# One token list instead of two in an attention, MLP and mixture-of-experts kernel, and three steps put elsewhere in its written order

## Chip, cores and metric

The kernel runs on one core of a Trainium2 chip, as one launch. The metric is the device time of one execution in microseconds (us); a lower time is better.

## Reference

Three layers follow one another on 4608 tokens of 512 numbers (8 sequences of 576 tokens, 8 heads of 64). The attention looks only inside chunks of 64 tokens.

```
scores = scale * q_c @ k_c^T;  attn = softmax(scores);  x = attn @ v_c      # chunks of 64
h = x @ w_in;  x = (s * relu(h)**2 + b) @ w_out                              # 512 -> 2048 -> 512
logits = x @ w_gate + modality_bias[modality_id];  e_idx = argmax(logits)
gate_w = softmax(logits)[e_idx]
for e in range(8):                                                           # 512 -> 1024 -> 512
    out[mask] = gate_w[mask] * (relu(x[mask] @ w1[e]) @ w2[e])
```

Everything is float32. The kernel reaches that precision by splitting numbers into a high and a low part and multiplying three times (high by high, high by low, low by high).

## The kernel before

**Tokens** go through attention and the first MLP in 18 blocks of 256 (`NB`), each two tiles of 128 (`NTB`). Blocks 0 and 1 run together in an opening stretch (functions `p_*`), in which the weights `w_in` and `w_out` also arrive and are split; blocks 2 to 17 run through `m_l1` (first matrix product) and `m_l2` (second), 16 column groups `f` each, the second two groups behind the first.

**The order is written by hand.** Inside `tc.manual_schedule` every engine executes its instructions in the order in which the Python code records them. An engine that waits for something therefore holds back all that was recorded behind it on that engine, ready or not. TensorE is PE in the profile, VectorE DVE, ScalarE ACT, GpSimd POOL; SyncE (SP) issues the ordinary DMAs.

**The opening.** Weight chunk `n` goes through `c_split` (ACT, two operations), `c_word` (DVE, three), `c_high` (ACT, writes the high part) and `c_low` (DVE, writes the low part). A token tile `i` goes through `a_transpose`, `a_scores`, `a_soft`, `a_norm`, `a_pt` and `a_pv`; `a_pv` multiplies by the values on PE (`pxt`), and ACT and DVE write the result's high and low part (`x`). After the hand-written opening a loop over steps `s` begins, whose step `s = 2` needs weight chunk 2 and, for its second half, tile 3's `x`.

**Choosing an expert.** For each block `j` `g_choose` (DVE, a dozen small operations ending in the one-hot `oh` and the running count `run`) takes the best of 8 logits. `g_rank` lets PE add up how many tokens chose each expert before (`prk`, five tiny products), `g_dest` (DVE) makes of it a row number, and `g_scatter` (POOL, two indirect DMAs, one for each token tile) writes each token's number into that row of a list in HBM. This is done one block behind, in group `f = 14` (`RANK`) and after it. For the last block the generator `routing()` does it, interleaved with the first expert units; its three steps are the logits' preparation, the choice, and then rank, scatter and the tables of units (`u_tables`, DVE).

**Two lists.** `ids` is a pair of lists, one for even and one for odd token tiles, with 8 x 4608 + 128 rows each. Both are filled with `HALF` = 2^19, and token t is written as t - 2^19; so the sum of the two entries of a row is the token's number, or 2^20 where no token is.

**Expert units.** A unit `u` is up to 128 tokens of one expert; units 0 to 3 are known early, and 41 units run here. `u_ids` (POOL) reads its 128 rows from both lists, `u_gather` (POOL) adds the two columns and gathers the tokens (`xg`), `u_x` transposes them on PE (`px`) and makes the scaled high and low parts on DVE (`scu`, `xf`, `xhl`), `u_l1(u, half)` is the first product (`pu`, with `hr` and `hh` behind it on DVE and ACT), `u_l2` the second (`po`), and an indirect DMA writes the rows (`out_dram`). `unit(u)` sets the order: `u_l1(u, 0)`, `u_x(u + 1)`, a step of `routing()`, `u_l1(u, 1)`, a step of `routing()`, gathers, `u_l2(u - 1)`. The scratch bank of PSUM that `px`, `plg` and `prk` use has two buffers.

The core of the order around the change:

```python
c_word(2); a_pv(3); c_high(2); c_split(3); p_relu(1); c_low(2)     # the opening
if f == RANK: g_rank(j - 1)                                        # blocks 2 to 16
l2_lag(j, f)
u_l1(u, 0); u_x(u + 1); next(route, None)                          # unit(u), u > 0
u_l1(u, 1); next(route, None)
```

Of the kernel before, what the change touches and what calls it, by code (L numbers as in the profile page):

```python
# [20 lines left out]


HALF = 1 << 19

# [6 lines left out]
def kernel(  # L31
# [58 lines left out]

    ids = [dram.tile([E * NT + P, 1], I32, name=f"ids{t}") for t in range(NTB)]
    wgt = dram.tile([E, DM], F32, name="wgt")
# [25 lines left out]
    tokid = const.tile([P, NTILE], I32, name="tokid")  # L118
    nc.gpsimd.iota(tokid, pattern=[[P, NTILE]], base=-HALF, channel_multiplier=1)
    eidx = iota("eidx", [P, E], [[1, E]])  # L120
# [37 lines left out]
    def small(n, shape, dt=F32, bufs=None):  # L158
        return sm.tile(shape, dt, tag=n, name=n, **({"bufs": bufs} if bufs else {}))
# [42 lines left out]
    def c_split(n):  # L202

        raw = craw[n]
        h, l = raw[:, :, 1], raw[:, :, 0]
        nc.scalar.activation(
            out=h.bitcast(F32), in_=h.bitcast(F32), func=AF.Copy, scale=2.0 ** -112
        )
        nc.scalar.activation(out=l, in_=l.bitcast(U32), func=AF.Copy, scale=2.0 ** -29)
# [24 lines left out]
    def c_low(n):  # L234
        hi, lo = c_dst(n)
        tt(lo, cwf.pop(n), hi.bitcast(F32), ALU.subtract)
# [421 lines left out]
    def g_scatter(j):  # L658
        di = rank.pop(j)
        for t in range(NTB):  # L660
            nc.gpsimd.indirect_dma_start(
                out=ids[t], out_offset=bass.IndirectOffsetOnAxis(ap=di[:, t, :], axis=0),
                in_=tokid[:, j * NTB + t:j * NTB + t + 1], in_offset=None,
            )
# [140 lines left out]
    def u_ids(u, idx):  # L805
        two = uid[u] = small("uid2", [P, NTB], I32, 6)
        for t in range(NTB):
            nc.gpsimd.indirect_dma_start(
                out=two[:, t:t + 1], out_offset=None, in_=ids[t],
                in_offset=bass.IndirectOffsetOnAxis(ap=idx, axis=0),  # L810
            )

    def u_gather(u):
        two = uid[u]
        uid[u] = small("uid", [P, 1], I32, 10)
        nc.gpsimd.tensor_tensor(out=uid[u], in0=two[:, 0:1], in1=two[:, 1:2], op=ALU.add)
        n = KNOWN_ROWS if u < NE else NT
        nc.gpsimd.indirect_dma_start(
            out=xg_t[u % 3], out_offset=None, in_=ys[:n],
            in_offset=bass.IndirectOffsetOnAxis(ap=uid[u], axis=0),  # L820
            bounds_check=n - 1, oob_is_err=False,
        )
# [284 lines left out]
    with tc.manual_schedule(engines=ENG):  # L1107
# [4 lines left out]
        none = su.tile([P, E * NTILE + 1], I32, tag="misc", name="none")  # L1112
        nc.vector.memset(none, HALF)
        a_load(0)
# [55 lines left out]
        c_word(2)  # L1170
        a_pv(3)
        c_high(2)
        c_split(3)
        p_relu(1)
        c_low(2)
        c_word(3)
# [6 lines left out]
        for s in range(2, NF + LEAD + LAG):  # L1183
# [44 lines left out]
            if s == 7:  # L1228
                nc.sync.dma_start(out=wg4, in_=w_gate.rearrange("(c p) e -> p c e", p=P))
                for t in range(NTB):  # L1230
                    nc.sync.dma_start(out=ids[t].rearrange("(p n) a -> p (n a)", p=P), in_=none)
            if s == 8:
# [38 lines left out]
    with tc.manual_schedule(engines=ENG):  # L1271
        for j in range(2, NB - 1):
            PREP, HIGH, STORE = PREP_2 if j == 2 else PREP5 if j < 8 else PREP4
            for f in range(NF):
                att_pe(j, f, 0)
                m_l1(j, f)
                att_pe(j, f, 1)
                if f == RANK:
                    g_rank(j - 1)
                l2_lag(j, f)  # L1280
                att_pe(j, f, 2)
                if f == (ROWS_2 if j == 2 else LAG - 1):
# [127 lines left out]
        def unit(u, lo, hi):  # L1410
            if u:
                u_l1(u, 0)
                if u + 1 < hi:
                    u_x(u + 1)
                next(route, None)
            u_l1(u, 1)
# [70 lines left out]
```

## Time and profile before

| | |
|---|---|
| Time, median of 3 runs | 1443.72 us (1437.5 to 1445.77) |
| Time of the profiled execution | 1438.02 us, span 1436.3 us |
| PE busy | 1394.2 us, 97% of the span |
| DVE busy | 1070.7 us, 75% |
| ACT busy | 724.1 us, 50% |
| POOL busy | 435.7 us, 30% |
| Granted PE clock, mean | 0.99 |

The span reaches from the first to the last instruction. An engine's row says how long it was executing; the rest it waited or had nothing to do. [...]

### The profile page before, as it was taken

The numbers are of one execution on the slowest core, as the hardware profiler recorded it, in microseconds if no ns is written. First come the engines' busy times: TensorE is split into PE (matmuls) and PEld (weight loads), VectorE is DVE, ScalarE is ACT, GpSimd is POOL, SyncE is SP. The second block draws the span as 40 slices with busy tenths as digits, with TensorE's granted clock in tenths as the row PEclk, the third lists the DMA queues.
The fourth block names the chain that finished last, engine by engine and source line by source line (L and its number), as shares of the span: only waits on it lengthen the run. The fifth ranks groups of instructions, "written<-read, shape, count | busy, mean of one in ns | idle before, by whom it ended". The sixth has DMA issues, their size and how long they took to land. (4 is left out here: it accounts for less than half of the span.)

```text
span 1436.3 us, 32039 instructions
## 1 busy us (share of the span) xinstructions
PE 1394.2 (97%) x11853; PEld 1151.0 (80%) x11853; DVE 1070.7 (75%) x2643; ACT 724.1 (50%) x1658; POOL 435.7 (30%) x515
## 2 busy tenths in 40 slices
PE   6899999999999999999999999998999999999995
PEld 5787888888888888888888888886767766776773
DVE  6987688877977977887697787767676676677662
ACT  4975555656565656655656565543233323333331
POOL 0000232332323333223323223463533433443320
PEclk9999999999999999999999999999999999999998
DMA  8673355555446443534534443461211231535340
GB/s 202 182 200 111 82 131 157 130 149 159 131 126 176 117 131 111 157 98 125 148 111 118 126 133 111 105 215 31 64 53 45 105 106 39 194 122 182 129 151 18
DMA packets 183886, 178.86 MB, mean 125 GB/s; under 512 B 131108, under 2 KB 139556, under 8 KB 179504
## 3 DMA queue, kind: packets, MB, share of 16 engines
q1 hardware_dynamic: 173392, 157.82, 37.7%
q0 software_dynamic: 10336, 18.97, 4.3%
q8 instruction: 95, 1.56, 0.5%
q14 instruction: 63, 0.52, 0.1%
HBM read 263.85 MB, written 54.14 MB: 221 GB/s over the span
## 5 line engine op out<-in xcount | busy, mean ns | idle before, releaser
L428 POOL TENSOR_TENSOR gl<-g,gh 128x256 fp32r<-128x256 f32 x256 | 221.6, 867 | 680.7 <-ACT gh L426 395.8
L413 PE MATMUL ph<-x,wi 128*128 128x256 f32 x2592 | 348.2, 285 | 5.0 <-ACT wi L232 3.8
L413 PEld LDWEIGHTS ph<-x,wi 128*128 128x128 f32 x2592 | 331.1, 190 | 20.2 <-ACT wi L232 4.4
L486 PE MATMUL py<-wo,gh 128*128 128x512 f32 x864 | 271.5, 395 | 0.2 <-DVE wo L166 0.2
L985 ACT ACTIVATE hr<-hr,scu 128x128 f32<-128x128 f32 x328 | 114.3, 396 | 282.0 <-DVE hr L166 262.4
L544 DVE CUSTOM_DVE_ANT_0 dump<-rows,wgb 128x512 bf16<-128x512 f32 x256 | 198.5, 775 | 5.0
L999 PEld LDWEIGHTS <-hh 128*128 128x128 f16 x984 | 95.0, 98 | 108.5 <-issue 2.2
L486 PE MATMUL py<-wo,gl 128*128 128x512 f32 x432 | 170.4, 395 | 0.0
L423 ACT ACTIVATE g<-ph 128x256 f32<-128x256 f32 x256 | 97.4, 380 | 136.1 <-PE ph L413 129.1
L486 PEld LDWEIGHTS py<-wo,gh 128*128 128x128 f32 x864 | 148.1, 188 | 21.8 <-DVE wo L166 0.5
L722 DVE SCALAR_TENSOR_TENSOR hl<-raw,wup,hl 128x512 f16<-128x512 f32 x128 | 111.1, 908 | 31.5 <-ACT hl L715 31.5
L973 PE MATMUL pu<-xhl,wa 128*128 128x256 f16 x736 | 127.9, 275 | 0.0
L977 PE MATMUL pu<-xhl,wa 128*128 128x128 f16 x736 | 125.4, 220 | 0.0
L999 PE MATMUL po<-wa,hh 128*128 128x512 f16 x552 | 124.6, 383 | 0.0
L715 ACT ACTIVATE hl<-raw,wup 128x512 f16<-128x512 f32 x128 | 85.5, 715 | 71.6 <-DVE wup L163 49.3
L413 PE MATMUL ph<-x,wj 128*128 128x256 f32 x864 | 116.7, 285 | 1.8 <-DVE wj L166 1.8
L981 DVE COPY hr<-pu 128x256 f32<-128x256 f32 x164 | 68.9, 420 | 61.5 <-PE pu L977 46.6
L1006 POOL DMA_INDIRECT out_dram<-o,uid x41 | 42.8, 1044 | 235.7 <-ACT o L1005 217.0
L413 PEld LDWEIGHTS ph<-x,wj 128*128 128x128 f32 x864 | 108.7, 189 | 6.3 <-DVE wj L166 2.0
L424 ACT ACTIVATE g<-g 128x256 f32<-128x256 f32 x256 | 107.5, 420 | 8.1
L426 ACT ACTIVATE gh<-g 128x256 fp32r<-128x256 f32 x256 | 107.4, 419 | 8.1
L973 PE MATMUL pu<-xhl,wb 128*128 128x256 f16 x576 | 98.9, 273 | 0.0
(216 smaller groups left out, 2271.9 us busy)
## 6 DMA issues: line engine op xcount, KB each, us to landing
wa<-wd SPq DMA_DIRECT2D x64, 1024.0 KB
wb<-wd SPq DMA_DIRECT2D x60, 1024.0 KB
raw<-in_moe_w_dram SPq DMA_DIRECT2D x64, 512.0 KB
wd<-hl SPq DMA_DIRECT2D x128, 256.0 KB
wb<-wd SPq DMA_DIRECT2D x20, 1030.5 KB
wa<-wd SPq DMA_DIRECT2D x20, 1030.5 KB
ys<-rows SPq DMA_DIRECT2D x18, 513.0 KB
vs<-in_v_dram SPq DMA_DIRECT2D x136, 64.0 KB
```

Source lines behind the costliest of these rows:

```text
L413: nc.tensor.matmul(ps, lhsT=wi_f(a, f)[:, kc], rhs=xt[j][b][:, kc, :], start=(n == 0), stop=(n == 3 * KC - 1),)
L423: nc.scalar.activation(out=g, in_=ps, func=AF.Relu)
L424: nc.scalar.activation(out=g, in_=g, func=AF.Square)
L426: nc.scalar.activation(out=hi, in_=g, func=AF.Copy)
L428: nc.gpsimd.tensor_tensor(out=lo, in0=g, in1=hi.bitcast(F32), op=ALU.subtract)
L486: nc.tensor.matmul(yps[j][t], lhsT=g[a][:, t * P:(t + 1) * P], rhs=wo_f(b, f), start=(f == 0 and n == 0), stop=(f == NF - 1 and n == 2),)
L544: nc.vector.tensor_tensor_reduce(out=dump, in0=ysb[j][:, t, :DM], in1=wgb[:, e * DM:(e + 1) * DM], scale=1.0, scalar=0.0, op0=ALU.mult, op ...
L722: nc.vector.scalar_tensor_tensor(out=hl[:, 1], in0=raw[:, a], scalar=sc, in1=hl[:, 0], op0=ALU.mult, op1=ALU.subtract)
L973: nc.tensor.matmul(ps[:, f], lhsT=w[:, kc, 0, cols], rhs=hl[:, :, kc, :], start=(kc == 0), stop=False,)
L977: nc.tensor.matmul(ps[:, f, 0], lhsT=w[:, kc, 1, cols], rhs=hl[:, 0, kc, :], start=False, stop=(kc == KC - 1),)
L985: nc.scalar.activation(out=r[:, f, :], in_=r[:, f, :], func=AF.Relu, scale=scu[:, c:c + 1])
L999: nc.tensor.matmul(ps, lhsT=hh[:, a, c, :], rhs=w[:, c % 4, b, :], start=(n == 0), stop=(n == 3 * NC2 - 1),)
```

## The change

Four edits. First, the two lists become one list `ids`, filled with 2^20 (`NONE`), and tokens are written under their own numbers; each token tile scatters through a view of its own (`dram_disjoint_views`), between which no order is kept, while a read of the list waits for the writes through both. So `u_ids` is one indirect DMA, and `u_gather`'s addition is gone. Second, in the opening weight chunk 2's `c_high`, `c_low` and chunk 3's `c_split` are recorded ahead of `a_pv(3)`. Third, at `j == 2` (block 1's rank) `g_rank` comes behind `l2_lag` and not ahead of it. Fourth, in unit 1 the choice step of `routing()` comes ahead of `u_x(2)`.

```diff
-    ids = [dram.tile([E * NT + P, 1], I32, name=f"ids{t}") for t in range(NTB)]
+    ids = dram.tile([E * NT + P, 1], I32, name="ids")
+    ids_v = dram_disjoint_views(ids, NTB)
...
-                out=ids[t], out_offset=bass.IndirectOffsetOnAxis(ap=di[:, t, :], axis=0),
+                out=ids_v[t], out_offset=bass.IndirectOffsetOnAxis(ap=di[:, t, :], axis=0),
...
     def u_ids(u, idx):
-        two = uid[u] = small("uid2", [P, NTB], I32, 6)
-        for t in range(NTB):
-            nc.gpsimd.indirect_dma_start(
-                out=two[:, t:t + 1], out_offset=None, in_=ids[t],
-                in_offset=bass.IndirectOffsetOnAxis(ap=idx, axis=0),
-            )
+        uid[u] = small("uid", [P, 1], I32, 10)
+        nc.gpsimd.indirect_dma_start(
+            out=uid[u], out_offset=None, in_=ids,
+            in_offset=bass.IndirectOffsetOnAxis(ap=idx, axis=0),
+        )
 
     def u_gather(u):
-        two = uid[u]
-        uid[u] = small("uid", [P, 1], I32, 10)
-        nc.gpsimd.tensor_tensor(out=uid[u], in0=two[:, 0:1], in1=two[:, 1:2], op=ALU.add)
...
         c_word(2)
-        a_pv(3)
         c_high(2)
         c_split(3)
+        c_low(2)
+        a_pv(3)
         p_relu(1)
-        c_low(2)
...
-                for t in range(NTB):
-                    nc.sync.dma_start(out=ids[t].rearrange("(p n) a -> p (n a)", p=P), in_=none)
+                nc.sync.dma_start(out=ids.rearrange("(p n) a -> p (n a)", p=P), in_=none)
...
-                if f == RANK:
+                if f == RANK and j > 2:
                     g_rank(j - 1)
                 l2_lag(j, f)
+                if f == RANK and j == 2:
+                    g_rank(j - 1)
...
             if u:
                 u_l1(u, 0)
+                if u == 1:
+                    next(route)
                 if u + 1 < hi:
                     u_x(u + 1)
-                next(route, None)
+                if u > 1:
+                    next(route, None)
             u_l1(u, 1)
```

ACT in the opening, from tile 3's `pt` on, before (`x` is tile 3's high part, `wi` weight chunk 2's, `craw` chunk 3's split, `wo` chunk 3's high part, `g` the first activation of step 1):

```order
L378 ACTIVATE pt<-ppt 128x512
L403 ACTIVATE x_484<-pxt 128x4x64 x2
L232 ACTIVATE wi_137<-wf 128x4x128
L206 ACTIVATE craw<-craw 128x512
L209 ACTIVATE craw<-craw 128x512
L450 ACTIVATE g<-ph 128x256
L232 ACTIVATE wo_129<-wf 128x512
```

and in the changed kernel:

```order
L379 ACTIVATE pt<-ppt 128x512
L233 ACTIVATE wi_136<-wf 128x4x128
L207 ACTIVATE craw<-craw 128x512
L210 ACTIVATE craw<-craw 128x512
L404 ACTIVATE x_483<-pxt 128x4x64 x2
L451 ACTIVATE g<-ph 128x256
L233 ACTIVATE wo_128<-wf 128x512
```

The two writes of `x` moved from ahead of three operations on weights to behind them. On DVE the low part of `wi` moved ahead of that of `x` in the same way.

DVE in unit 1, between the two halves of its first product, before (`scu`, `xf`, `xhl` are unit 2's tokens, `lg` to `run` the last block's choice):

```order
L166 TENSOR_TENSOR hh<-hr,hh 128x512
L948 COPY scu<-wa_12873 128x13
L166 TENSOR_TENSOR scu<-scu,xg_12869 128x1
L166 TENSOR_TENSOR xf<-px,scu 128x512
L956 CAST xhl<-xf 128x512
L166 TENSOR_TENSOR xhl<-xf,xhl 128x512
L568 COPY lg<-plg 128x16
...
L594 TENSOR_REDUCE first<-eq 128x2
L166 TENSOR_TENSOR oh<-rev_94,first 128x16
L166 TENSOR_TENSOR run<-run,oh 128x8 x2
L981 COPY hr<-pu 128x256
```

and in the changed kernel:

```order
L167 TENSOR_TENSOR hh<-hr,hh 128x512
L569 COPY lg<-plg 128x16
...
L595 TENSOR_REDUCE first<-eq 128x2
L167 TENSOR_TENSOR oh<-rev_93,first 128x16
L167 TENSOR_TENSOR run<-run,oh 128x8 x2
L945 COPY scu<-wa_12871 128x13
L167 TENSOR_TENSOR scu<-scu,xg_12867 128x1
L167 TENSOR_TENSOR xf<-px,scu 128x512
L953 CAST xhl<-xf 128x512
L167 TENSOR_TENSOR xhl<-xf,xhl 128x512
L978 COPY hr<-pu 128x256
```

The choice and unit 2's tokens changed places; what stands ahead of and behind the two together is the same. On PE the products `plg` and the transposes `px` changed places.

POOL from the last block's scatter to the gather of unit 4's tokens, before (`ids_73`, `ids_74` are the two lists, `uid_13878` and `uid_13881` the columns of units 4 and 5):

```order
L661 DMA ids_73<-tokid,di 36992x1
L661 DMA ids_74<-tokid,di 36992x1
L808 DMA uid_13878<-ids_73,gidx 128x1
L808 DMA uid_13878<-ids_74,gidx 128x1
L808 DMA uid_13881<-ids_73,gidx 128x1
L808 DMA uid_13881<-ids_74,gidx 128x1
L816 TENSOR_TENSOR uid<-uid_13878 128x1
L818 DMA xg_12868<-ys,uid 128x513
```

and in the changed kernel, with the two instructions that follow:

```order
L662 DMA ids<-tokid,di 36992x1 x2
L808 DMA uid<-ids,gidx 128x1 x2
L815 DMA xg_12866<-ys,uid 128x513
L808 DMA uid<-ids,gidx 128x1
L1003 DMA out_dram<-o,uid 4608x512
```

Between the scatter and unit 4's gather stand two instructions now where there were five.

## Rows read from the trace of the kernel before

**Rows 1.** The page, its first part: engine, busy us, share of the span, instructions.

```profile
PE 1394.2 (97%) x11853; PEld 1151.0 (80%) x11853; DVE 1070.7 (75%) x2643; ACT 724.1 (50%) x1658; POOL 435.7 (30%) x515
```

**Rows 2.** Waits of PE: line and releaser, total us, times, longest us.

```profile
PE ph L413 <- DVE wj L166: 1.8, 1, 1.8
```

**Rows 3.** Stretches: length, busy us of each engine, granted clock, DMA share, GB/s.

```profile
30.00:35.00 5.00, 4.59 (x48) 4.18 (x48) 2.40 (x5) 0.97 (x3) 0.00 (x0) 0.50 0.77 268
...
216.00:970.00 754.00, 753.06 (x6462) 667.15 (x6461) 591.35 (x1547) 440.72 (x1013) 248.87 (x286) 1.00 0.48 135
...
981.00:984.00 3.00, 3.00 (x8) 1.03 (x7) 2.17 (x10) 2.71 (x7) 0.00 (x0) 0.50 0.01 3
...
1004.50:1007.50 3.00, 3.00 (x22) 2.40 (x20) 2.86 (x7) 0.00 (x0) 2.03 (x4) 0.50 0.38 107
1008.00:1424.00 416.00, 413.46 (x3450) 288.88 (x3448) 278.55 (x630) 131.37 (x339) 150.30 (x178) 1.00 0.30 103
```

**Rows 4.** Timeline of ACT, opening: start us, duration us, operation, idle before and releaser.

```profile
34.63 0.66 ACT L403 ACTIVATE x<-pxt 128x256 fp32r<-128x256 f32 x2 [3.02 <-PE pxt L391]
...
36.81 0.38 ACT L450 ACTIVATE g<-ph 128x256 f32<-128x256 f32 x1
```

**Rows 5.** Timeline of DVE, opening.

```profile
31.88 0.69 DVE L219 SCALAR_TENSOR_TENSOR wf<-craw,wf 128x512 int32<-128x512 int32 x1
35.04 0.76 DVE L166 TENSOR_TENSOR x<-pxt,x 128x256 fp32r<-128x256 f32 x2 [2.48 <-ACT x L403]
35.84 0.69 DVE L166 TENSOR_TENSOR wi<-wf,wi 128x512 fp32r<-128x512 f32 x1
36.45 0.42 DVE L163 TENSOR_SCALAR wf<-craw 128x512 int32<-128x512 int32 x1
```

**Rows 6.** Timeline of PE around block 1's rank.

```profile
193.17 0.17 PE L635 MATMUL prk<-run,ones 128*128 128x8 bf16 x1 [1.17 <-DVE x L166]
...
193.27 0.71 PE L486 MATMUL py<-wt,gh 128*128 128x512 f32 x2
...
194.74 1.46 PE L413 MATMUL ph<-x,wj 128*128 128x256 f32 x11
```

**Rows 7.** Timeline of DVE, units 1 to 3.

```profile
976.22 0.17 DVE L948 COPY scu<-wa 128x13 f32<-128x13 f32 x1
...
978.28 0.17 DVE L568 COPY lg<-plg 128x16 f32<-128x16 f32 x1
...
979.52 0.18 DVE L166 TENSOR_TENSOR oh<-rev,first 128x16 bf16<-128x16 f32 x1
...
980.01 0.42 DVE L981 COPY hr<-pu 128x256 f32<-128x256 f32 x1
...
996.43 0.69 DVE L166 TENSOR_TENSOR xhl<-xf,xhl 128x512 f16<-128x512 f32 x1
```

**Rows 8.** Timeline of PE, units 1 to 4.

```profile
979.75 0.17 PE L636 MATMUL prk<-oh,tri 128*128 128x8 bf16 x1 [2.35 <-DVE oh L166]
...
980.17 7.03 PE L999 MATMUL po<-wa,hh 128*128 128x512 f16 x24
...
992.75 5.34 PE L999 MATMUL po<-wa,hh 128*128 128x512 f16 x24
...
997.93 0.27 PE L973 MATMUL pu<-xhl,wa 128*128 128x256 f16 x1
...
1003.19 0.66 PE L952 MATMUL px<-ident,xg 128*128 128x128 f32 x4 [2.45 <-DMA xg<-ys,uid]
...
1007.98 5.34 PE L999 MATMUL po<-wa,hh 128*128 128x512 f16 x24
```

**Rows 9.** Timeline of POOL, last scatter to unit 4's gather.

```profile
994.04 1.10 POOL L808 DMA_INDIRECT uid<-ids,gidx  x1 [7.11 <-DMA ids<-tokid,di]
...
996.82 1.12 POOL L808 DMA_INDIRECT uid<-ids,gidx  x1 [0.30 <-issue]
...
999.69 1.11 POOL L818 DMA_INDIRECT xg<-ys,uid  x1 [0.27 <-issue]
```

More of the change, by code (lines that the diff above doesn't have):

```diff
@@ L6 @@
 from concourse._compat import with_exitstack
+from concourse.ap import dram_disjoint_views
 from concourse.masks import make_identity
@@ L20 @@
 EXP_MASK = 0x7F800000
-HALF = 1 << 19
+NONE = 1 << 20
 def pow2(n):
@@ L118 @@
     tokid = const.tile([P, NTILE], I32, name="tokid")
-    nc.gpsimd.iota(tokid, pattern=[[P, NTILE]], base=-HALF, channel_multiplier=1)
+    nc.gpsimd.iota(tokid, pattern=[[P, NTILE]], base=0, channel_multiplier=1)
     eidx = iota("eidx", [P, E], [[1, E]])
@@ L1112 @@
         none = su.tile([P, E * NTILE + 1], I32, tag="misc", name="none")
-        nc.vector.memset(none, HALF)
+        nc.vector.memset(none, NONE)
         a_load(0)
```

## Prediction

> **What bounds the kernel now.** I read the page first: PE is busy 97% of the span, 1394.2 of 1436.3 us [rows 1]. So there are only 42 us to be had without removing products, and a gain must come out of single waits of PE, or out of stretches in which PE runs at half clock. The view of stretches shows where those are. From 216 to 970 us PE is busy 753 of 754 us, and from 1008 to 1424 413 of 416 at full clock [rows 3]; there PE sets the time, and whatever is won ahead of it is kept to the end. The waits lie in the opening, around block 1's rank, and where the last block's choice meets the first expert units. [...] What such a stretch costs is seen on one pair: the same 24 products of `u_l2` took 7.03 us across the first of them and 5.34 us at full clock [rows 8], so 1.69 us. The timelines of the three places then tell which engine is late.
>
> **The opening.** ACT waits 3.02 us for tile 3's products and DVE 2.48 us for ACT [rows 4, 5], while chunk 2's word is ready since 31.88 + 0.69 = 32.57 [rows 5]. In the changed order ACT and DVE make chunk 2's parts in that idle time. `x` still comes at 34.63 and 35.04, when PE has made it, and behind it DVE goes on to chunk 3 at 35.84 and not at 36.45 [rows 5]: 0.6 us earlier. PE is earlier there by more, but DVE is what it waits for next; it waits for DVE again at the end of the stretch (1.8 us for `wj` [rows 2]), so DVE's 0.6 us is the gain. The other bound: PE ran this stretch at half clock [rows 3]. Had it run at full clock, its 4.59 busy us would have been up to 2.3 us shorter and `x` ready by 32.3. ACT, in the new order, would not be free for it then: the operations on weights that now stand ahead take 36.81 - 34.63 - 0.66 = 1.5 us [rows 4] from 32.6 on, so `x` would come at 34.1. DVE would reach chunk 3 at 34.1 + 1.2 = 35.3, where the old order had 32.3 + 1.8 = 34.1. So -0.6 to +1.2; I take -0.6, since this trace has the half clock there, and what stands ahead of it is not changed.
>
> **Block 1's rank.** PE stands 1.17 us until `x` on DVE has let go of the scratch buffer and `run` is there, at 193.17 [rows 6]. Now six products of `l2_lag` come first, 194.74 - 193.27 = 1.47 us [rows 6], and the rank finds its inputs ready: -1.2. The destination on DVE has that much less lead, but nobody on PE waits for it. Behind it PE has under 1 us of idle time up to 970 [rows 3]; if being ahead makes it meet DVE again, up to all of it goes back. So -1.2 to 0; I take -1.2.
>
> **The choice ahead of unit 2's tokens.** On DVE the choice takes 979.52 + 0.18 - 978.28 = 1.42 us up to `oh` and begins at 976.22 in place of 978.28 [rows 7], so `oh` is there at 977.64. PE goes on 2.06 us earlier: `u_l2(0)` starts at 978.1 and not at 980.17 [rows 8], and as the wait falls to some 0.7 us, the half clock behind it should not come: 1.69 us more. That would be 3.75 us. But it isn't kept. The choice and the tokens have only changed places on DVE; at 980.01 DVE is where it was [rows 7], and everything behind is as late as before, the scatter and the tables of units as well. PE would come to `u_l1(3, 0)` at 997.93 - 3.75 = 994.2, and its operand `xhl` of unit 3 ends on DVE at 996.43 + 0.69 = 997.12 [rows 7]. So PE gets a new wait of some 3 us there, starts at 997.2, and has won 0.76 us. These products last until 1003.19 - 2.45 = 1000.74, 2.81 us from 997.93 [rows 8]; now they end at 999.98.
>
> **One list.** POOL reads the list from 994.04 on, once the scatter has landed [rows 9]; with two lists unit 4's gather came after four reads and an addition, at 999.69. With one list it comes in the third slot, 996.82 [rows 9], if its own column has landed by then. No row shows that landing alone; unit 4's gather, which moves 513 times as much, was there 1003.19 - 999.69 = 3.50 us after its start [rows 8, 9], so the column is there between at once and 997.54. The tokens follow 3.5 us later: at 1000.3 to 1001.1, I take 1000.6. Elsewhere 41 reads and 41 additions fewer on POOL cost and gain nothing: POOL is idle 70% of the time [rows 1], and only unit 4's gather is waited for. The fill that SP no longer issues was one transfer behind work; nothing.
>
> **The clock.** PE is at `px` of unit 4 at 999.98, just ahead of the tokens. But it has waited 3 us on the way, longer than the two waits that half clock followed [rows 8]; I count 1.69 us for the new wait. Then PE comes to `px` at 1001.7, after the tokens, and from there to `u_l2(2)` it needs 1007.98 - 1003.19 - 1.69 = 3.10 us [rows 8]. `u_l2(2)` starts at 1004.8 in place of 1007.98: -3.2. Without the half clock it would be 1000.6 + 3.1 = 1003.7, so -4.3; with late tokens (1001.1) and the half clock behind them 1001.1 + 4.8 = 1005.9, so -2.1. [...]
>
> **The sum.** -0.6 - 1.2 - 3.2 = -5.0 us. Against the profiled execution: span 1436.3 to 1431.3, time 1438.02 to 1433.0. That execution stands 5.7 us under the median of the three runs, which lie between 1437.5 and 1445.77; I take the change off the median: 1443.72 - 5.0 = 1438.7. About 0.5%, 7.2 us, is what a measurement of this kernel can tell from no change.
>
> **The rivals.** *All that was waited for is won.* If unit 3's operand is not late, both waits and both half-clock stretches go: 0.6 + 1.2 + 2.06 + 1.69 + 2.45 + 1.69 = 9.7, 1434.0 from the median. For it: PE is the bound before and behind. Against it: `xhl` of unit 3 on DVE, which no edit moves [rows 7]. *The old waits come back.* ACT holds tile 3's `x` in an execution with full clock there, or PE meets DVE again behind the rank: 3.2 - 1.2 = 2.0 won, 1441.7. For it: ACT's written order; against it: half clock in this trace [rows 3]. The same figure holds if the list changes nothing: unit 4's gather waiting for its own column until the old 999.69 leaves 0.6 + 1.2 + 0.8 = 2.6. *The one list is slower to write, and the kernel slower.* Two scatters now put 256 numbers of 4 bytes into neighbouring rows of one list, with no order between them, and POOL's next read waits for both. Its wait was 7.11 us [rows 9]. Up to 1.1 us more stays hidden, since PE comes at 1001.7; past that each us costs one, and the new wait for tokens brings back 1.69. Were the wait twice as long, the tokens came at 1007.7, 6.0 + 1.7 = 7.7 worse than the forecast, and the kernel were 2.7 us slower than before: 1446.4. It turns slower than before from some 4.4 us of extra landing. Against it: both scatters were in flight together before as well. [...]
>
> **How the numbers follow.** The forecast gets 0.60, all won 0.12, the old waits 0.16, the slower list 0.08, and 0.04 is left for what I don't see. The predicted time is the forecast's, 1438.7. The range starts with the profiled execution's base less 7 (the forecast without half clock, 6.1, and a part of the first rival): 1431; it ends at the median of before, 1444, which takes in the old waits; what is outside is most of the slower list and the rest of the first rival. A gain over 0.5% comes from the first rival (0.10) and from the forecast where the spread of the runs, 8 us, adds 2 us to it (0.20): 0.30. A loss over 0.5% needs the list far slower: 0.06. The rest, 0.64, is within.
>
> **What would show it.** Right: PE waits about 0.7 us at `prk` of the last block and none at block 1's; a new wait of about 3 us at the first half of unit 3's product, released by DVE's `xhl`; unit 4's gather on POOL three slots behind the scatter, 2.9 us after the first read; PE's wait for `xg` under 1 us or gone; DVE in the opening 0.6 us ahead from chunk 3 on. Wrong: no wait at unit 3 (then DVE had slack that I don't see), POOL's wait behind the scatter well over 8 us, or ACT's `x` in the opening behind a finished `pxt`.

## The result and the profile after

The changed kernel takes 1418.86 us (median of 4 runs, 1418.59 to 1419.1), the kernel before 1442.28 us (median of 4 in the same job, 1437.5 to 1445.77): ratio 0.984, 95% interval 0.981 to 0.987. The prediction was 1438.7 us, its range went from 1431 to 1444. Between the medians 23.4 us are won, where the forecast had 5.0. The profiled executions, 1438.02 and 1418.85 us, are 19.2 us apart, and the traces say where. The first part of the page of after:

```profile
PE 1383.1 (98%) x11853; PEld 1143.7 (81%) x11853; DVE 1067.9 (75%) x2643; ACT 720.8 (51%) x1658; POOL 390.9 (28%) x433
```

PE's instructions are as many as before [rows 1], but it is busy 11.1 us less. That is the first sign of something unforeseen: the edits take waits away, and of busy time only what half clock (granted 0.50 [rows 3]) had added behind them. What that is worth is measured once: the 24 products at 980.17, which cross 981 to 984 at 0.50, took 7.03 us and those at 992.75 5.34 [rows 3, 8], so 1.69 us.

To divide the 19.2 us I take points that both programs pass: `rows` on DVE (a block's second product read out) of block 0, block 2 and the last block, 17, the last output tile `o` on ACT, and the end of the span. In the timeline of before:

```profile
143.89 1.40 DVE L495 SCALAR_TENSOR_TENSOR rows<-py,sb,cb 128x512 f32<-128x512 f32 x2
...
204.35 1.46 DVE L495 SCALAR_TENSOR_TENSOR rows<-py,sb,cb 128x512 f32<-128x512 f32 x2 [4.41 <-PE py L486]
...
614.63 1.45 DVE L495 SCALAR_TENSOR_TENSOR rows<-py,sb,cb 128x512 f32<-128x512 f32 x2 [4.39 <-PE py L486]
665.67 1.45 DVE L495 SCALAR_TENSOR_TENSOR rows<-py,sb,cb 128x512 f32<-128x512 f32 x2 [4.40 <-PE py L486]
...
966.02 1.41 DVE L495 SCALAR_TENSOR_TENSOR rows<-py,sb,cb 128x512 f32<-128x512 f32 x2
...
1421.55 0.69 ACT L1005 ACTIVATE o<-po,scu 128x512 f32<-128x512 f32 x1 [4.54 <-PE po L999]
```

and of after:

```profile
143.22 1.41 DVE L496 SCALAR_TENSOR_TENSOR rows<-py,sb,cb 128x512 f32<-128x512 f32 x2
...
202.35 0.75 DVE L496 SCALAR_TENSOR_TENSOR rows<-py,sb,cb 128x512 f32<-128x512 f32 x1 [3.58 <-PE py L487]
...
609.39 1.45 DVE L496 SCALAR_TENSOR_TENSOR rows<-py,sb,cb 128x512 f32<-128x512 f32 x2 [4.34 <-PE py L487]
659.77 1.45 DVE L496 SCALAR_TENSOR_TENSOR rows<-py,sb,cb 128x512 f32<-128x512 f32 x2 [4.34 <-PE py L487]
...
957.16 1.40 DVE L496 SCALAR_TENSOR_TENSOR rows<-py,sb,cb 128x512 f32<-128x512 f32 x2
...
1408.73 0.69 ACT L1002 ACTIVATE o<-po,scu 128x512 f32<-128x512 f32 x1 [4.54 <-PE po L996]
```

| stretch | before | after | difference | forecast |
|---|---|---|---|---|
| start to block 0's rows | 143.89 | 143.22 | -0.67 | -0.6 |
| to block 2's rows (block 1's rank) | 60.46 | 59.13 | -1.33 | -1.2 |
| to block 17's rows | 761.67 | 754.81 | -6.86 | 0 |
| to the last output tile (choice, list, units) | 455.53 | 451.57 | -3.96 | -3.2 |
| to the end of the span | 14.75 | 8.37 | -6.38 | 0 |

The three places that the forecast worked out came within 0.8 us. The other 13.2 us lie where it had nothing: in the blocks up to 17, where PE had no idle time to lose, and behind the last output tile. The two middle rows of each timeline are two consecutive late blocks: 51.04 us before, 50.38 after. Below, "a late block" is such a difference; over blocks 9 to 15 it repeats in one kernel within 0.04 us, except in one run. Fifteen blocks at 0.67 us would be 10 us. This pair has 6.9, since the first six and the last two of them are less regular: their lengths differ by about 1 us between kernels in which the late blocks are alike.

Most of what makes a block shorter is in the products of the first layer. PE's costliest group before and after (count, busy us, mean ns of one):

```profile
L413 PE MATMUL ph<-x,wi 128*128 128x256 f32 x2592 | 348.2, 285 | 5.0 <-ACT wi L232 3.8
```

```profile
L414 PE MATMUL ph<-x,wi 128*128 128x256 f32 x2592 | 343.4, 283 | 2.9 <-ACT wi L233 2.5
```

Same products, same operands `x` and `wi`, and 2 ns less for each; in the stretch of the blocks the granted clock is 1.00 before [rows 3] and after (214 to 961 us).

The forecast places themselves. PE's waits of after:

```profile
PE pu L970 <- DVE xhl L167: 3.0, 1, 3.0
PE ph L414 <- ACT wi L233: 2.5, 1, 2.5
PE ph L414 <- DVE wj L167: 1.8, 1, 1.8
...
PE prk L637 <- DVE oh L167: 0.5, 1, 0.5
```

The wait for `oh` fell from 2.35 us [rows 8] to 0.5, the wait for unit 4's tokens is gone, and there is a new wait of 3.0 us for unit 3's `xhl`. PE behind them:

```profile
968.13 0.17 PE L637 MATMUL prk<-oh,tri 128*128 128x8 bf16 x1 [0.54 <-DVE oh L167]
...
968.54 5.34 PE L996 MATMUL po<-wa,hh 128*128 128x512 f16 x24
...
987.79 0.40 PE L970 MATMUL pu<-xhl,wa 128*128 128x256 f16 x1 [3.01 <-DVE xhl L167]
992.08 0.61 PE L949 MATMUL px<-ident,xg 128*128 128x128 f32 x4
```

The 24 products at 968.54 take 5.34 us and not 7.03 [rows 8]: no half clock behind the wait of 0.54 us. Behind the new one there is, as the stretches of after show (length, busy us by engine, granted clock, DMA share, GB/s):

```profile
985.00:987.80 2.80, 0.01 (x1) 0.01 (x1) 2.70 (x7) 0.00 (x0) 1.82 (x2) 1.00 0.01 0
987.80:991.20 3.40, 3.40 (x22) 2.72 (x23) 2.54 (x6) 1.96 (x5) 2.36 (x3) 0.50 0.29 81
991.20:995.00 3.80, 3.80 (x47) 3.55 (x46) 2.67 (x7) 1.39 (x4) 2.26 (x3) 1.00 0.41 136
```

In the opening DVE comes from chunk 2's word to chunk 3 in 35.67 - 31.83 = 3.84 us, where it took 36.45 - 31.88 = 4.57 [rows 5]; `x` is where it was, and `wi` now lies in the idle time ahead of it:

```profile
31.83 0.69 DVE L220 SCALAR_TENSOR_TENSOR wf<-craw,wf 128x512 int32<-128x512 int32 x1
33.22 0.69 DVE L167 TENSOR_TENSOR wi<-wf,wi 128x512 fp32r<-128x512 f32 x1 [0.69 <-ACT wi L233]
35.00 0.76 DVE L167 TENSOR_TENSOR x<-pxt,x 128x256 fp32r<-128x256 f32 x2 [1.09 <-ACT x L404]
35.67 0.42 DVE L164 TENSOR_SCALAR wf<-craw 128x512 int32<-128x512 int32 x1
```

### The profile page after: what moved, and what is told of

Same layout as the page of the kernel before. It is cut to its first block, busy times and chain, and to the rows that moved or that the text cites. A ratio compares the mean times of both kernels' runs of the same rounds, so it can differ in the third digit from the quotient of the medians.

```text
span 1417.1 us, 31878 instructions
## 1 busy us (share of the span) xinstructions
PE 1383.1 (98%) x11853; PEld 1143.7 (81%) x11853; DVE 1067.9 (75%) x2643; ACT 720.8 (51%) x1658; POOL 390.9 (28%) x433
## 5 line engine op out<-in xcount | busy, mean ns | idle before, releaser
L429 POOL TENSOR_TENSOR gl<-g,gh 128x256 fp32r<-128x256 f32 x256 | 226.2, 886 | 671.6 <-ACT gh L427 406.3
L414 PE MATMUL ph<-x,wi 128*128 128x256 f32 x2592 | 343.4, 283 | 2.9 <-ACT wi L233 2.5
L414 PEld LDWEIGHTS ph<-x,wi 128*128 128x128 f32 x2592 | 327.0, 190 | 17.4 <-ACT wi L233 2.9
```

Of the source, the lines that this page charges most:

```text
L414: nc.tensor.matmul(ps, lhsT=wi_f(a, f)[:, kc], rhs=xt[j][b][:, kc, :], start=(n == 0), stop=(n == 3 * KC - 1),)
L429: nc.gpsimd.tensor_tensor(out=lo, in0=g, in1=hi.bitcast(F32), op=ALU.subtract)
```

## The experiments

**The suspicion about blocks 2 to 17.** `u_ids` had two columns per unit in six small buffers `uid2` of 32 bytes a partition. They are gone, and every buffer behind the pool of small tiles stands 192 bytes lower in SBUF: among them wt, rows, dump, wgb, g, gh, gl, raw and hl. `x` (ahead of that pool) and `wi`, `wj`, `wo` (at the far end) have not moved. Theory: the place of moved buffers sets the pace. Rivals: the list itself does, or the new order of work.

*pad192.* In the changed kernel's `u_ids`:

```
+        pad = small("pad", [P, NTB], I32, 6)
         uid[u] = small("uid", [P, 1], I32, 10)
```

> The changed kernel with 192 unused bytes put back into the pool of small tiles, where the second list's columns stood; every buffer behind it lies at its old address, and nothing else differs. The theory of addresses (the first-layer products of blocks 2 to 17 run faster because buffers behind that pool moved by 192 bytes): a block takes 51.05 us again in place of 50.37, so about 6.8 us come back over ten blocks and more: 1425.8. The theory that the edits themselves did it (by the list, or by the order of work): 1418.9, a block at 50.37. The end of the program, from the last output tile on ACT to the end of the span, stays 8.4 us by both, since POOL issues the same 159 indirect transfers.

*list_only*: the diff's first edit alone.

> The kernel before with the one list alone; opening, block 1's rank and the choice stand as before. Its buffers lie where the changed kernel's do. Theory of addresses, and the rival that the list itself sets the pace: blocks at 50.37 us, 6.9 us won there, and 6.4 us at the end of the program, so 1442.3 - 13.3 = 1429. The rival that the other three edits set the pace of the blocks: blocks at 51.05, only the end is won: 1435.9.

*list_undone*: the other three edits alone.

> The changed kernel with its two lists back, so that only the opening, block 1's rank and the choice differ from before. Its buffers lie at the old addresses, and POOL issues 200 indirect transfers. Theory of addresses, and the rival that the list itself sets the pace: 51.05 us a block and 14.8 us from the last output tile to the end; only the forecast's 0.6 + 1.2 + 0.8 are won: 1439.7. The rival that the three edits set the pace: 50.37 us a block, 1432.8.

*before_pad64.* In the `u_ids` of the kernel before:

```
         two = uid[u] = small("uid2", [P, NTB], I32, 6)
+        pad = small("pad", [P, NTB], I32, 2)
```

> The kernel before with 64 unused bytes added to the pool of small tiles: the buffers behind it then stand where the changed kernel has them within a line of 256 bytes, 256 bytes further on, and no other instruction differs. Theory of addresses, if the place within 256 bytes decides: 50.37 us a block, 1442.3 - 6.9 = 1435.4. If it is another part of the address, or the edits: 51.05 us a block, 1442.3. The end stays 14.8 us by all, with 200 indirect transfers.

The four ran in one job, where the kernel before had 1438.19 us (median of 13):

| kernel | median us | ratio, 95% interval | late block | last tile to end |
|---|---|---|---|---|
| pad192 | 1430.62 | 0.995, 0.9933 to 0.9966 | 51.05 | 8.2 |
| list_only | 1422.81 | 0.9902, 0.9886 to 0.9919 | 50.37 | 8.7 |
| list_undone | 1435.62 | 0.9983, 0.9974 to 0.9993 | 51.05 | 14.3 |
| before_pad64 | 1428.64 | 0.9938, 0.9921 to 0.9954 | 50.37 | 14.3 |

The late block follows the place in all four, whatever the edits. Nine late blocks seen from the first to the last `rows` (count, ns, first and last start) in pad192:

```profile
L496 DVE SCALAR_TENSOR_TENSOR rows<-py,sb,cb x18: 750/752/755, 513.0 to 920.3; 128x512 f32<-128x512 f32 x18
```

and in before_pad64:

```profile
L495 DVE SCALAR_TENSOR_TENSOR rows<-py,sb,cb x18: 750/751/753, 508.8 to 910.8; 128x512 f32<-128x512 f32 x18
```

407.3 us against 402.0: (407.3 - 402.0) / 8 = 0.66 us a block. 64 unused bytes, not one instruction changed, make the kernel before 9.6 us faster in the median. And both rivals fall: list_only has the fast block without the new order, pad192 the slow one with list and order. The end goes with the list alone. list_undone shows the forecast without the list, 0.6 + 1.2 + 0.8 = 2.6 us: measured 1438.19 - 1435.62 = 2.6. The totals expected for the other three were off by 5 to 7 us: the kernel before stood 4.1 us lower in this job than the figure they started from, the place was worth 9.6 us in the median and not 6.9, and in pad192 the tokens of unit 4 came late again (see the account below).

**Which buffer.** Further kernels differ from before only in unused bytes inside the pools:

```
 g_p, _ = pool("g", 3, st=ctx)
+g_p.tile([P, 16], F32, tag="pad", name="pad", bufs=1)    pad_g
...
 pp, pp_st = pool("pp")
+pp.tile([P, 16], F32, tag="pad", name="pad", bufs=1)     pad_pp
...
+if (j, f) == (2, 0):                                     pad_gh; ahead of lo: pad_gl
+    g_p.tile([P, 16], F32, tag="pad", name="pad", bufs=1)
 hi = g_p.tile([P, TB], F32R, tag="gh", name="gh")
```

gl32 and gl128 are pad_gl with 8 and 32 numbers in place of 16. `raw` and `hl` lie behind these buffers and move along; pad_pp moves them alone.

*pad_g.*

> The kernel before with 64 unused bytes ahead of the buffers g, gh and gl: these and the buffers behind them (raw, hl) move by 64 bytes, while wt, rows, dump and wgb stay. If it is the place of g, gh, gl, raw or hl that slows the first-layer products, a late block takes 50.37 us, as with all buffers moved by 64; if it is wt, rows, dump or wgb, 51.05 us as before. The end stays at 14.3 to 14.8 us.

*pad_pp.*

> The kernel before with 64 unused bytes ahead of raw and hl alone, the staging buffers for the expert weights, which DMA fills and DVE and ACT read. If their place slows the products, a late block takes 50.37 us; if it is that of g, gh and gl, or of the buffers ahead, 51.05 us.

*pad_gh.*

> The kernel before with 64 unused bytes between g and gh: gh and gl (and raw and hl behind them, which cost nothing alone) move, g stays. Moving g, gh and gl together brought a late block from 51.05 to 50.56 us. If the place of g slows the products, it is 51.05 here; if that of gh or gl, 50.56.

*pad_gl.*

> The kernel before with 64 unused bytes between gh and gl: only gl (with raw and hl) moves; POOL writes it and PE loads it as weights of the second product. If gl's place alone slows the products, a late block takes 50.56 us; if gh's, or both have to be moved, 51.05.

*gl32.*

> The kernel before with gl alone moved by 32 bytes, to 224 over a multiple of 256, where wi and wo start too. If a start at a multiple of 64 is what makes it fast, the late block is 51.05 us or longer; if any place other than 192 over is fast, 50.4; if the place counts relative to that of the other operands, a third value.

*gl128.*

> The kernel before with gl alone moved by 128 bytes, to 64 over a multiple of 256. If a start at a multiple of 256 is what makes it fast, the late block stays at 51.05 us; if any place other than 192 over, 50.4; if the place counts relative to that of the other operands, a third value.

**POOL's writing or PE's reading.** `gl` is the low part of the hidden values: POOL writes it, PE loads it as weights of the second product. Two kernels leave that low part out: `gl` is written once, with zeros, and PE goes on loading it.

```
-        lo = g_p.tile([P, TB], F32R, tag="gl", name="gl")
-        nc.gpsimd.tensor_tensor(out=lo, in0=g, in1=hi.bitcast(F32), op=ALU.subtract)
-        gch[j, f] = (hi, lo)
+        if not low:
+            for n in range(3):
+                low.append(g_p.tile([P, TB], F32R, tag=f"gl{n}", name=f"gl{n}", bufs=1))
+                nc.gpsimd.tensor_tensor(out=low[n], in0=g, in1=g, op=ALU.subtract)
+        gch[j, f] = (hi, low[f % 3])
```

nolo_new has pad_gl's 64 bytes ahead of these buffers as well.

*nolo_old.*

> The kernel before without the low part of g: gl is written once with zeros and then only loaded by PE, from its old address, so POOL's 867 ns subtraction is gone from each product group of blocks 2 to 17. If POOL's accesses there slow PE's first-layer products, a late block falls from 51.05 us to 50.4 or less; if PE's own loading of gl from this place does it, it stays at 51.05.

*nolo_new.*

> The same without the low part of g, with gl 64 bytes further on. If POOL's accesses are the cause, the place no longer matters: the same block as in the run with the old place. If PE's loading is the cause, the block is shorter than there by the 0.67 us that moving gl won.

**Whether a multiple of 256 is the rule.** Unused bytes in the changed kernel:

```
+px_p, _ = pool("padx", st=ctx)
+px_p.tile([P, 24], F32, name="padx")                     align_x, align_all
 xt_p, _ = pool("xt", 2, st=ctx)
...
+pr_p, _ = pool("padr", side="right", st=ctx)
+pr_p.tile([P, 56], F32, name="padr")                     align_all
 wo_p, wo_st = pool("wo", side="right")
...
+        pad = small("pad", [P, NTB], I32, 5)             align_x, align_all
         uid[u] = small("uid", [P, 1], I32, 10)
```

*align_x.*

> The changed kernel with 96 unused bytes ahead of x and 160 behind: x starts at a multiple of 256 bytes in place of 160 over one, gl and the rest stay at a multiple of 256. If the place of what PE reads paces the products (x is the moving operand of the first layer), a late block falls from 50.37 us by about as much again, 0.7; if only what POOL and PE share matters, 50.37.

*align_all.*

> As that, with 224 unused bytes at the far end as well, so that wi, wj, wo and the opening's g, gh and gl, all 224 bytes over a multiple of 256, start at multiples too. If PE's weights and the second layer's moving operand are paced by their place, blocks fall below those with x alone; the two-block opening, whose products run at the slow pace in both kernels, falls by up to 2.0 us (some 380 products by 4 to 5 ns). If not, 50.37 us and the opening as before.

All of them in one table: bytes over a multiple of 256 at which each buffer starts in the built program, and the late block (`wt` is the last quarter of `w_out`, which PE reads in the second product as it does `wo`):

| kernel | x | wi, wj, wo | wt | g | gh | gl | late block, us |
|---|---|---|---|---|---|---|---|
| before, pad192, list_undone, pad_pp | 160 | 224 | 160 | 192 | 192 | 192 | 51.05 |
| pad_gl | 160 | 224 | 160 | 192 | 192 | 0 | 50.38 |
| gl32 | 160 | 224 | 160 | 192 | 192 | 224 | 50.86 |
| gl128 | 160 | 224 | 160 | 192 | 192 | 64 | 50.75 to 50.79 |
| pad_gh | 160 | 224 | 160 | 192 | 0 | 0 | 50.56 |
| pad_g | 160 | 224 | 160 | 0 | 0 | 0 | 50.56 |
| after, list_only, before_pad64 | 160 | 224 | 224 | 0 | 0 | 0 | 50.37 |
| nolo_old (no low part) | 160 | 224 | 160 | 192 | 192 | 192 | 51.05 |
| nolo_new (no low part) | 160 | 224 | 160 | 192 | 192 | 0 | 50.38, but once 51.04 and then 49.72 |
| align_x | 0 | 224 | 224 | 0 | 0 | 0 | 50.88 |
| align_all | 0 | 0 | 224 | 0 | 0 | 0 | 51.14 |

The staging buffers raw and hl cost nothing (pad_pp, 51.05). Moving `gl` alone gives the whole gain, and four places of `gl` give four paces. The nine late blocks of pad_gl:

```profile
L497 DVE SCALAR_TENSOR_TENSOR rows<-py,sb,cb x18: 749/752/755, 510.5 to 912.6; 128x512 f32<-128x512 f32 x18
```

pad_g and before_pad64 differ in the buffers ahead of g, worth 0.19 us; of these PE reads only `wt` in the late blocks, but moving that alone wasn't tried. POOL is cleared, as nolo_old shows: its row for `gl` (count, busy us, mean ns, idle before) and its nine late blocks:

```profile
L432 POOL TENSOR_TENSOR gl<-g 128x256 fp32r<-128x256 f32 x3 | 1.8, 612 | 145.5 <-ACT g L426 145.5
L499 DVE SCALAR_TENSOR_TENSOR rows<-py,sb,cb x18: 750/752/756, 511.7 to 919.1; 128x512 f32<-128x512 f32 x18
```

3 subtractions are left of 256, and the late block is 51.05 us as with all of them; moving `gl` is worth the same with and without POOL's work, 51.05 - 50.38 = 0.67 us a block. Only POOL and PE touch `gl`, so what is left is that PE loads it from there. But starting at a multiple of 256 is no rule: `x` moved to one costs 0.51 us a block, and with `x`, `wi`, `wj`, `wo`, `g`, `gh` and `gl` at one (`wt` alone is not) the block is the longest, 51.14 us. The opening of align_all is no shorter either: block 0's rows come at 143.21 us, where the changed kernel has 143.22.

By what law the places count stays open: whether each buffer's place has a price of its own, or the places count relative to each other, no run separates. Nor is it shown why `ph`, which does not read `gl`, is the group that slows most (280 ns a product on `wi` in pad_gl between 560 and 900 us, 283 in before). It is not only the products right behind the loads of `gl`: `ph` comes in runs of 12, and in the late blocks the last four products of a run on `wi`, over 1 us behind the last load of `gl`, start 117.2 ns apart in before and nolo_old, 114.4 in pad_gl and nolo_new, 113.3 in after and 119.5 in align_all.

The total times of these runs, one each, are not compared, since they differ in other places: in pad_gh and pad_gl PE also stood between products in units 2 and 3 (some 4 us), by the profile for nothing but "issue", and had 6.8 us of half clock there. These runs gave 1437.85 (pad_gh), 1435.85 (pad_gl), 1433.39 (gl32), 1432.99 (gl128), 1432.71 (pad_g), 1437.29 (pad_pp), 1438.08 and 1431.27 (nolo), 1427.49 (align_x) and 1430.29 us (align_all).

**The end of the program.** Behind the last output tile the kernel has little to do; the view of the last line of before shows who is last (count, ns least/median/most, first and last start):

```profile
L1483 SPq EVENT_SEMAPHORE  x14: 17/28/28, 1427.7 to 1436.2; - x14
L1483 POOLq EVENT_SEMAPHORE  x4: 17/17/17, 1435.5 to 1436.2; - x4
L1483 POOLq DRAIN  x3: 40/107/7742, 1427.7 to 1436.0; - x3
```

and of after:

```profile
L1484 SPq EVENT_SEMAPHORE  x14: 17/28/28, 1411.8 to 1417.1; - x14
L1484 POOLq EVENT_SEMAPHORE  x4: 17/17/17, 1416.4 to 1417.0; - x4
L1484 POOLq DRAIN  x3: 40/107/4393, 1411.9 to 1416.9; - x3
```

SPq and POOLq are the instruction streams of SP and POOL; DRAIN is one of the instructions on the program's last line. The longest DRAIN on POOL takes 7.742 us before and 4.393 after. POOL has issued 200 indirect transfers before, 159 after. Four kernels change that number, three by repeating the read of a unit's column into spare numbers of the same 32-byte buffer:

```
-        uid[u] = small("uid", [P, 1], I32, 10)
-        nc.gpsimd.indirect_dma_start(
-            out=uid[u], out_offset=None, in_=ids,
+        ten = small("uid", [P, 8], I32, 10)
+        uid[u] = ten[:, 0:1]
+        for c in range(2):                              reads200
+        for c in range(5 if u >= NU - 30 else 1):       reads271
+        for c in range(3 if u >= NU - 30 else 1):       reads215
+            nc.gpsimd.indirect_dma_start(
+                out=ten[:, c:c + 1], out_offset=None, in_=ids,
```

and one in the blocks:

```
                 if f == SCATTER:
                     g_scatter(j - 1)
+                if f in (3, 7, 11, 15)[:4 if j < 11 else 3]:
+                    nc.gpsimd.indirect_dma_start(
+                        out=small("spare", [P, E], F32, 8), out_offset=None, in_=w_gate,
+                        in_offset=bass.IndirectOffsetOnAxis(ap=tokid[:, 0:1], axis=0),
+                    )
```

*reads200.*

> The changed kernel with each read of a unit's column done twice, the second time into a spare column beside it that nobody uses: 200 indirect transfers on POOL as before, the one list, every address and the rest as in the changed kernel. If the length of the program's end follows the number of indirect transfers that POOL has issued, it is back at 14.3 to 14.8 us from the last output tile, and SyncE's wait behind the last instruction at 7.2 us in place of 3.3. If it follows the additions, the second list or the addresses, it stays at 8.4. The blocks stay at 50.37 us.

*reads271.*

> The changed kernel with four further reads of the column for each of the 28 last units, into spare columns that nobody uses: 271 indirect transfers. If the end grows by each transfer as from 159 to 200 (6.2 us for 41, 0.15 each), it is 8.4 + 112 x 0.15 = 25 us; if only up to a limit of what may be outstanding, it is between 8 and 15.

*reads215.*

> The changed kernel with two further reads of the column for each of the 28 last units: 215 indirect transfers. The end was the same at 200 transfers in every kernel (SyncE's last wait 7.2 us) and at 159 (3.3), but at 271 it was between (4.3). A count that starts again every 106 transfers fits all three: 53, 94 and 59 left over. By it 215 leave 3 over, SyncE's last wait is about 0 and the end 4 to 5.5 us from the last output tile. If the wait only grows and then levels off, or goes by the time since the last transfers, it is 4.3 to 8 us and the end 10 to 15.

*early213.*

> The changed kernel with 54 small indirect reads that nobody uses, one at a time on POOL inside blocks 2 to 16, where it is idle two thirds of the time: 213 indirect transfers in all. Buffers move by 256 bytes, so a late block should stay at 50.37 us. If the end goes by the number of transfers that is left over 212, it is about 4 us shorter than the changed kernel's 8.4, and the kernel comes to 1418.9 - 4 = 1415; if the end grows with the number, 1418.9 + 7 = 1426. A cost of the reads themselves on the blocks would show as blocks over 50.37.

| transfers | kernels | longest DRAIN on POOL, us | last tile to end, us |
|---|---|---|---|
| 159 | after, pad192, list_only, align_x, align_all | 4.393 | 8.2 to 8.8 |
| 200 | before and all its variants, reads200 | 7.742 | 14.3 to 15.2 |
| 213 | early213 | 8.803 | 14.4 |
| 215 | reads215 | 8.967 | 16.7 |
| 271 | reads271 | 4.883 | 11.2 |

That the DRAIN goes by the number of transfers is shown for 159 to 215: reads200 has the changed kernel's one list, addresses and additions, and before's DRAIN to the nanosecond. From 159 to 215 each transfer adds (8.967 - 4.393) / 56 = 0.082 us. My count that starts again every 106 fell: 213 and 215 should have been near zero. Why 271 is low stays open; a count that starts again only somewhere between 216 and 271 isn't excluded.

Of the 6.4 us, 41 x 0.082 = 3.35 are the DRAIN. The other 3.0 lie ahead of it (it starts 6.2 us behind the last tile before, 3.2 after), and the traces split them. POOL's last instruction ahead of the DRAIN is, before and after:

```profile
L1443 POOLq INC_SWDGE_SEM  x1: 2067/2067/2067, 1425.6 to 1425.6; - x1
```

```profile
L1444 POOLq INC_SWDGE_SEM  x1: 1269/1269/1269, 1410.6 to 1410.6; - x1
```

It goes by the number too: 2.067 us at 200 transfers (2.070 in reads200), 1.269 at 159, 2.345 at 213, 2.370 at 215. So 3.35 + 0.80 = 4.1 of the 6.4 us are shown to be the transfers' number. Most of the rest, 1.7 us, is one wait: before, POOL waits until 1425.56 for the last rows to land and then starts this instruction; after, it starts it at 1410.63, while the last rows land at 1412.54. That this wait goes with the number isn't shown: early213, with 213 transfers, starts it ahead of the landing as well, so that its end, 14.4 us, is shorter than that of reads200 (15.2) with its shorter DRAIN.

The median of early213 is 1436.64 us, ratio to before 0.9972 (0.9959 to 0.9985): its late blocks stay at 50.37, as 256 bytes of shift let expect, but with the extra reads each of the five stretches from block 2's rows to block 7's is 1.2 to 2.3 us longer than in the changed kernel (PE waits 6.9 us there for `rows`). In reads271 PE stood another 13 us for "issue". So these reads, for which nobody waits, were not free either; why wasn't tried. reads200, reads215 and reads271, run once each, took 1434.61, 1438.27 and 1443.89 us.

No version of these beats the changed kernel.

## Why the prediction was wrong, and where it was right

**What failed** is one sentence under "One list": "Elsewhere 41 reads and 41 additions fewer on POOL cost and gain nothing: POOL is idle 70% of the time, and only unit 4's gather is waited for." It failed twice. The program's end waits for POOL, whose last DRAIN and the instruction ahead of it took longer with more transfers issued, up to 215 of them: of the 6.4 us won, 4.1 by these two, and most of the rest by a wait for the last rows. And the reads' buffers went too, which moved `gl` to a place from which PE works faster: 6.9 us in the profiled pair, 9.6 in the median of before_pad64. The first paragraph drew the false comfort: "there PE sets the time, and whatever is won ahead of it is kept to the end" takes the length of a full stretch as given. PE busy 753 of 754 us [rows 3] says that nobody else holds PE up, not that its products run as fast as they can.

**The opening**: -0.67 for -0.6, by the step foreseen; that the size fits is luck, since block 0's rows come between 142.6 and 145.5 us in the twenty profiles, 0.4 us earlier in the mean of nine with the new order than of eleven with the old one. The other bound, a loss of up to 1.2 us where PE has full clock there, was wrong in sign. From chunk 2's word to chunk 3 DVE took 3.91 and 3.83 us in list_only and before_pad64, which keep the old order, and 3.46 in list_undone and pad192 with the new one; PE had its full clock in all four where it made tile 3's `x` (granted 1.00 in the last 1.2 us ahead of `x` on DVE). So 0.4 us are won there too. ACT did hold `x` back, as that bound has it (in list_undone `x` starts at 35.51, 0.5 us behind the end of tile 3's products), but DVE, which has the low part of `wi` ahead of `x` now, comes to chunk 3 sooner all the same.

**Block 1's rank**: -1.33 for -1.2, and no wait went back. From block 1's rows to block 2's the old order took 38.01 to 38.27 us in nine profiles (before, list_only, before_pad64 and the six kernels that move single buffers), the new one 36.64 to 36.96 in eight (early213, with its extra reads, and the two without the low part are left aside).

**The choice**: right in each part. The wait for `oh` is 0.54 us (0.7 foreseen), the half clock behind it is gone, and the new wait for `xhl` is 3.0 (3 foreseen).

**One list and the clock**: -3.96 for -3.2 in this pair, more by luck than the forecast knew. The gather of unit 4 stands in the third slot, as foreseen; it starts 988.23 - 984.78 = 3.45 us behind the first read, not 2.9, since it waits 1.10 us for its column (the profile says "issue"; by the semaphore events the column landed at 987.48), on POOL of after:

```profile
984.78 0.98 POOL L808 DMA_INDIRECT uid<-ids,gidx  x1 [7.40 <-DVE hh L986]
986.06 1.06 POOL L808 DMA_INDIRECT uid<-ids,gidx  x1 [0.31 <-issue]
988.23 1.01 POOL L815 DMA_INDIRECT xg<-ys,uid  x1 [1.10 <-issue]
```

The rival of the slower list is half true. POOL's wait behind the last scatter is 6.2 to 7.1 us in eleven profiles with two lists (mean 6.5) and 7.4 to 8.9 in nine with one (mean 8.3): the first read is 1.8 us later. (The release that the row above names, DVE's `hh`, is a coincidence; the scatters' semaphores came last, at 983.92.) Only half of that is slower landing. With two lists the first read needs the first list's scatter alone; with one it needs both, and the second scatter starts 1.3 us later. By the semaphore events the second scatter had landed 6.5 us behind its end with two lists in the mean (6.3 to 7.0) and 7.4 with one (6.5 to 8.0): 0.9 us. Why it lands later in one list, no run shows. The prediction had the wait for both and gave it no price. After's 7.40 is the shortest of its nine, and PE waited 1.2 to 2.7 us for unit 4's tokens in six of these nine. In pad192, with 8.83, PE waited 2.7 us for the tokens again, and from block 17's rows to the sixth output tile it took 78.85 us, where after took 76.09 and before 80.04. The delay stayed far under the 4.4 us from which the kernel would have been slower.

The clock differs from execution to execution. list_only had waits of 2.35 us for `oh` and 1.84 for the tokens, at the places of before, and no half clock behind either:

```profile
968.10:972.50 4.40, 1.92 (x23) 1.61 (x21) 4.16 (x18) 0.00 (x0) 0.00 (x0) 1.00 0.15 41
985.00:1000.00 15.00, 12.44 (x99) 8.13 (x98) 12.20 (x29) 4.74 (x13) 8.12 (x9) 1.00 0.22 70
```

Before had it (granted 0.50 [rows 3]) behind both, 2.35 and 2.45 us [rows 8]. All eleven profiles with the old order of the choice have that wait of 2.35 us for `oh`; the 24 products behind it took 6.66 to 7.03 us in five of them and 5.34 in six. So half clock behind the same wait cost up to 1.69 us in some executions and nothing in others; what decides it, no trace shows. The 1.69 us that the forecast put behind the new wait came true in after (granted 0.50 from 987.80 to 991.20), but that it would come was an estimate: behind the wait of 2.35 us both outcomes were measured.

## What to carry to other kernels

An edit that removes a buffer can also move all that is allocated behind it (here by 192 bytes, 0.67 us a late block), and an edit that removes indirect transfers can also shorten what the program's end waits out (here 41 transfers, 4.1 us); look for both in the built program before calling such an edit free. A stretch in which an engine is busy all the time is not a constant: compare the mean duration of its instructions (here 285 and 283 ns), and where PE is the bound, try a few dozen unused bytes ahead of its operands, one buffer at a time, and measure, since no rule for the best place came out of these runs. Before crediting a change with a gain, run it once with the old addresses put back.

## What the runs showed of the hardware

- A late block took 51.05, 50.86, 50.77 or 50.38 us by the place of `gl` in SBUF alone (before, gl32, gl128, pad_gl: 192, 224, 64 and 0 bytes over a multiple of 256), and 51.05 and 50.38 again with POOL's writes of `gl` left out (nolo_old, nolo_new). The last four products of a run on `wi`, over 1 us behind the last load of `gl`, started 117.2 or 114.4 ns apart. With all but one of the operands at multiples of 256 bytes (align_all) the block was the longest, 51.14.
- POOL's last DRAIN took 4.393, 7.742, 8.803 and 8.967 us behind 159, 200, 213 and 215 indirect transfers (after, before, early213, reads215), 0.082 us for each, but 4.883 behind 271 (reads271); the instruction ahead of it took 1.269, 2.067, 2.345 and 2.370 us behind 159 to 215.
- Of two scatters of 128 numbers each, the second one landed 6.5 us behind its end when each had a list of its own and 7.4 us when they shared one, in the mean of eleven and nine profiles.
- Behind the same wait of 2.35 us for `oh` PE's 24 products took 6.66 to 7.03 us in five profiles and 5.34 in six; the granted clock was 0.50 from 981 to 984 us in before and 1.00 from 968.1 to 972.5 in list_only.
